# Whole 128-token chunks for group 0's attention, and group 2's attention moved to units 12 to 16

## The chip, the cores and the metric

The kernel runs on one core of one Trainium2 chip. The metric is the device time of one execution in microseconds. Before the change the median of three runs is 645.27 us (644.62 to 645.66).

Names of engines: PE (TensorE), ACT (ScalarE), DVE (VectorE), POOL (GpSimd), SP (the queue that issues nearly all DMAs). All five work through their own list of instructions strictly in order, and wait for each other by semaphores.

## The reference

Inputs: q, k, v of shape (4 batches, 8 heads, 768 positions, 64), a decay `lam` per head, and the weights of a gated layer. First a blocked linear attention with a running state, then RMS norm, then the gated layer:

```python
for b in range(nb):                       # blocks of 64 positions
    intra = (qb @ kb.T) * Dmask           # Dmask[i, j] = lam ** (i - j) for i >= j, else 0
    out = intra @ vb + (qb * lam ** (i + 1)) @ kv_state
    kv_state = lam ** 64 * kv_state + (kb * lam ** (63 - i)).T @ vb
x = out as (3072 tokens, 512)
xn = x / sqrt(mean(x * x) + 1e-6) * rms_g
y = (silu(xn @ w_gate) * (xn @ w_val)) @ w_out      # d_ff = 1536
```

The result does not depend on the block length: blocks of 128 positions with lam ** 128 between them compute the same.

## The kernel before

The 3072 tokens are six groups (m = 0 to 5) of 512. A group has four pairs of heads (p = 0 to 3), each pair filling the 128 partitions, and the layer's 1536 columns are twelve blocks of 128 (f). A unit is one group times one block: `gate` and `val` products into PSUM, silu and a multiplication, a split of the hidden values into a high and a low part, and `out` products into four accumulators. Units 0 to 5 are (0, f < 6), 6 to 17 are group 1, 18 to 23 are (0, f >= 6); from unit 24 on groups 2 to 5 run with a Strassen scheme (`strassen`, matmuls of L987), which needs sums of the group's rows (`Norm.sums`) and of the weights (`WeightSums`).

Before a group's units come its attention and its norm. The attention of one pair (class `Pair`) computes with 64x64 tiles, two blocks of 64 (o = 0, 1) in each chunk of 128 tokens:

- `scores` (L524, 16 matmuls), then `decay_a` on DVE (L540) multiplies with the mask, `decay_k` on ACT (L531) and `decay_q` on POOL (L544) scale k and q;
- `mix_chunks` (L604, 16 matmuls) and `state_sums` (L554, 16 matmuls);
- the states of the two blocks of a chunk are joined: `decay_sums` on ACT (L570), `whole_sums` on DVE (L573), `chain` over the chunks on DVE (L579), `middle` on DVE (L585), and `turn` on ACT (L592), which copies the halves across partitions;
- `mix_states` (L622, 14 to 16 matmuls), `keep_output` (L636, two ACT copies), `keep_squares` (L645).

Groups 0 and 1's attention and the conversion of the first seven weight blocks form the ramp. There the scheduler puts matmuls of `busy` (L141, tile `unread`) into PE's list wherever it expects a hole; they compute nothing. Group 0's norm (`row_sums` L667, `root` L691 on POOL, `spread` L700, `scaled` L753, `high` L758, `low` L761) ends in the first product of unit 0 (L800). Group 2's attention stands in units 16 to 19 of the list of steps, its norm in unit 21, and the scores of group 3's first pair in unit 23.

The order of all engines is made by a planner (`Plan.run`) at build time: every step has an engine, a cost, an `at` in units, what it reads and writes and which buffers it opens; a table `SHIFTS` moves the `at` of single steps. The planner lists the steps, and the emitted programs follow that list.

Loads of q, k, v and of weights share four buffers of 1 MB (`in`); from unit 24 on two of them hold the Strassen operands (`operand_tiles`). The group's rows x are kept in two buffers x0 and x1 (`SLOT_OF`).

Of the kernel before, what the change touches and what calls it, by code (L numbers as in the profile page):

```python
# [23 lines left out]
def retention_swiglu_kernel(  # L24
# [50 lines left out]
    lams, gcol = (cs[:, :NP], cs[:, NP : 2 * NP]), cs[:, 2 * NP :]  # L75
# [37 lines left out]
    pending = [(load_qkv, 1, 0), (load_gv, 1)]  # L113
# [42 lines left out]
    diagonal = const.tile([P, D], F32, name="diagonal")  # L156
    nc.gpsimd.tensor_add(diagonal, ident[:, :D], ident[:, D:])

    def powers(p, part):
        for s in range(2):  # L160
            lam = lams[s][:, p : p + 1].broadcast_to([P, D])
            if part == s:
                nc.vector.tensor_tensor_scan(
                    mask[:, p, s, :], lam, diagonal, 0.0, ALU.mult, ALU.add
                )
            elif part == 2:
                nc.vector.tensor_tensor_scan(
                    pw[:, p, s, :], lam, zeros, 1.0, ALU.mult, ALU.add
                )
        if part == 2:  # L170
            one = pw[:, p, 0, D - 1 :]
            nc.vector.tensor_mul(both[:, p : p + 1], one, one)
# [48 lines left out]
    zeros = wg[:, NF - 1, 1].bitcast(F32)[:, :D]  # L221
    nc.scalar.mul(zeros, ones[:, :D], 0.0)
# [272 lines left out]
    rows = {}  # L495
    xs = {}

    class Pair:
# [3 lines left out]
        def __init__(self, m, p):  # L502
            self.m, self.p = m, p
            if m == 0 and p % 2 or m == 1 and p == 0:
                self.pool, self.banks = ps_out, ("po0", "po1")
            elif m in (1, 2):
# [67 lines left out]

        def chain(self, chunks):
            for c in chunks:
                if c < GC - 1 and self.starts(c + 1):
# [3 lines left out]
                    both[:, self.p : self.p + 1], self.pst[1][:, c], ALU.mult, ALU.add,  # L581
# [45 lines left out]
        def keep_output(self, eng=nc.scalar):  # L627
            m, p = self.m, self.p
            if m not in rows:
                x = xpool.tile([P, NK, G], F32, tag=f"x{SLOT_OF[m]}", name=f"x_{m}")  # L630
                rows[m] = x, []
            x = rows[m][0]
# [15 lines left out]
        def add_squares(self, eng):  # L648
            sums = rows[self.m][1]
            s1 = sums.pop(1)  # L650
            eng.tensor_add(sums[0], sums[0], s1)

# [240 lines left out]

    def operand_tiles():
# [213 lines left out]
    units += [(m, f) for m in range(2, NG) for f in range(NF)]  # L1108
    SLOT_OF = {m: m % 2 if m < 2 else (m + 1) % 2 for m in range(NG)}
# [6 lines left out]
    class Plan:  # L1116
# [9 lines left out]
        SINGLE = {"row_sums", "spread", "quick", "largest_of_all"}  # L1126
# [4 lines left out]
            "quick": 16, "gate": 8, "val": 8, "part": 10, "out": 6, "add": 12, "first": 12, "second": 12,  # L1131
# [256 lines left out]
    def scale_steps(i, at):  # L1388
        step("DVE", 0.95, at, row_scales, slice(i * HALF, (i + 1) * HALF), w=[f"ts{i}"])

    def halve_steps(f, at):
# [7 lines left out]
        step("POOL", 1.28, at + 0.2, h.low, r=[f"rl{f}", f"rh{f}"], w=[f"w16_{f}:o"])  # L1399

    def sum_steps(f, at):
# [3 lines left out]
        for i in range(2):  # L1405
            step("POOL", 1.15, at + 0.1 * i, s.whole, i, tag, r=[f"w{'vg'[i]}{f}"], w=[f"r{f}:{i}"],
                 new=[] if i else [(f"r{f}", tag)])
        for i in range(2):
            step("DVE", 0.84, at + 0.5 + 0.1 * i, s.sums, i, to, r=[f"r{f}:0", f"r{f}:1"], w=[f"ws{f}"],
# [77 lines left out]

    def pair_scores(q, at):
# [511 lines left out]
```

## Time and profile before

| | us |
|---|---|
| median of three runs | 645.27 |
| the profiled execution | 644.94 |
| its span, first to last instruction | 643.2 |
| PE busy | 626.6 (97%) |
| DVE busy | 442.8 (69%) |
| ACT busy | 361.0 (56%) |
| POOL busy | 160.8 (25%) |

The span begins with the first instruction and ends with the landing of the last output; 1.7 us of the execution lie around it. Busy means that an instruction of the engine is under way. PE counts as busy in filler matmuls too. An idle time before an instruction is shown in square brackets with what ended it.

### The profile page before, as it was taken

What the parts mean: (1) busy time and instruction counts of PE and PEld (TensorE: products, weight loads), DVE (VectorE), ACT (ScalarE), POOL (GpSimd) and SP (SyncE); (2) the same over time, 40 slices, a digit from 0 to 9 for tenths busy, and PEclk for the clock granted to TensorE, in tenths of its full rate; (3) what the DMA queues carried; (4) which work ended last, traced back from release to release, by engine and by line L of the source; (5) the groups of instructions that cost most, each with busy time, mean ns of one, the idle gap of its engine ahead of it and who ended that gap; (6) DMA issues with size and microseconds to landing.
All of it is one profiled execution on the core that took longest, in us unless ns stands there. A gap on an engine that the chain in (4) does not pass through costs nothing.

```text
span 643.2 us, 15795 instructions
## 1 busy us (share of the span) xinstructions
PE 626.6 (97%) x6614; PEld 421.5 (66%) x6614; DVE 442.8 (69%) x892; ACT 361.0 (56%) x772; POOL 160.8 (25%) x166
## 2 busy tenths in 40 slices
PE   8899999999999999899999999999999999999997
PEld 5645564555556555677776777777777777777774
DVE  6698988789879867976678554498454488433434
ACT  4788877666856564465635455536454545433342
POOL 3213122000466763566601201112110102000000
PEclk9999999999999999999999999999999999999999
DMA  8738662540102400321200311200220000100001
GB/s 323 282 120 281 244 229 99 196 131 26 41 1 59 141 2 1 115 84 42 93 2 2 116 52 48 97 22 2 89 84 28 2 2 1 63 4 1 1 1 67
DMA packets 14327, 51.35 MB, mean 80 GB/s; under 512 B 1712, under 2 KB 1968, under 8 KB 12848
## 3 DMA queue, kind: packets, MB, share of 16 engines
q1 hardware_dynamic: 13968, 50.21, 22.5%
q8 instruction: 52, 0.85, 0.5%
q14 instruction: 19, 0.16, 0.1%
q10 hardware_dynamic: 288, 0.14, 0.1%
HBM read 44.05 MB, written 6.29 MB: 78 GB/s over the span
## 4 chain that ended last, share of the span: by engine, by line
PE 83%; DVE 9%; ACT 3%; issue 2%; DMA 1%; POOL 0%; DVEq 0%; ACTq 0%
PE pa L987 19%; PE pb L987 14%; PE acc L819 9%; PE acc L821 9%; PE acc L820 9%; PE pg L800 8%; PE pv L800 8%; PE pa L524 2%; PE po L604 2%; PE po L622 2%; PE po L554 1%; DVE a L579 1%; DVE x L761 1%; DVE a L540 1%; DMA qkv<-in_qkv_dram 1%
## 5 line engine op out<-in xcount | busy, mean ns | idle before, releaser
L821 PE MATMUL acc<-wo,hh 128*128 128x512 f16 (+1 forms) x288 | 110.2, 383 | 0.0
L820 PE MATMUL acc<-wo,hh 128*128 128x512 f16 (+1 forms) x288 | 110.1, 382 | 0.0
L1035 ACT COPY tx<-pa 128x256 f32<-128x256 f32 x144 | 53.1, 369 | 89.5 <-PE pa L987 66.0
L819 PE MATMUL acc<-wo,hh 128*128 128x512 f16 x216 | 82.0, 380 | 0.1
L1039 DVE TENSOR_TENSOR tx<-pb,tx 128x256 f32<-128x256 f32 x96 | 40.7, 424 | 56.0 <-PE pb L987 53.1
L800 PE MATMUL pv<-x,wv 128*128 128x512 f16 x288 | 69.0, 379 | 1.1 <-DVE sg L1068 1.1
L800 PE MATMUL pg<-x,wg 128*128 128x512 f16 x288 | 68.2, 379 | 0.9 <-ACT sg L1061 0.4
L987 PEld LDWEIGHTS <-wg 128*128 128x128 f16 x576 | 56.3, 98 | 17.8
L1080 ACT CAST hh<-sg 128x512 f16<-128x512 f32 (+2 forms) x73 | 44.6, 611 | 37.4 <-DVE sg L1055 25.4
L987 PEld LDWEIGHTS <-wo 128*128 128x128 f16 x576 | 55.8, 98 | 14.6 <-issue 1.3
L987 PEld LDWEIGHTS <-wv 128*128 128x128 f16 x576 | 56.1, 98 | 12.4 <-issue 1.2
L1043 DVE TENSOR_TENSOR sg<-pb,tx 128x256 f32<-128x256 f32 x48 | 20.3, 423 | 44.9 <-ACT tx L1035 34.1
L1091 DVE TENSOR_TENSOR hh<-sg,hh 128x512 f16<-128x512 f32 x53 | 43.1, 813 | 11.1 <-ACT hh L1080 10.9
L800 PEld LDWEIGHTS <-wg 128*128 128x128 f16 x288 | 27.1, 98 | 33.6 <-issue 2.1
L1055 DVE SCALAR_TENSOR_TENSOR sg<-tx,cv,sg 128x512 f32<-128x512 f32 (+1 forms) x49 | 38.0, 775 | 15.8 <-ACT sg L1047 12.2
L800 PEld LDWEIGHTS <-wv 128*128 128x128 f16 x288 | 26.5, 97 | 32.7 <-issue 2.3
L1047 ACT ACTIVATE sg<-sg,cg 128x256 f32<-128x256 f32 x48 | 24.4, 508 | 37.7 <-DVE sg L1043 37.6
L987 PE MATMUL pa<-x,wv 128*128 128x256 f16 x288 | 39.5, 273 | 0.9 <-DVE a L540 0.6
L987 PE MATMUL pb<-x,wv 128*128 128x256 f16 x288 | 39.4, 273 | 0.7 <-DVE x L761 0.7
L544 POOL TENSOR_TENSOR qkv<-qkv,pw 128x512 f32<-128x512 f32 x24 | 32.6, 1357 | 30.3 <-PE pa L524 28.1
L987 PE MATMUL pb<-tx,wo 128*128 128x256 f16 x288 | 39.3, 273 | 0.2 <-DVE tx L1039 0.2
L987 PE MATMUL pa<-x,wg 128*128 128x256 f16 x288 | 39.3, 273 | 0.0
(194 smaller groups left out, 1192.1 us busy)
## 6 DMA issues: line engine op xcount, KB each, us to landing
qkv<-in_qkv_dram SPq DMA_DIRECT2D x48, 512.0 KB, 5.2
raw_gv<-in_weights_dram SPq DMA_DIRECT2D x11, 1024.0 KB, 6.0
raw_o<-in_weights_dram SPq DMA_DIRECT2D x12, 512.0 KB, 5.0
out_dram<-o SPq DMA_DIRECT2D x23, 256.0 KB, 2.1
partial<-in_weights_dram SPq DMA_DIRECT2D x2, 512.0 KB, 11.9
out_dram<-o SPq DMA_DIRECT2D x1, 128.0 KB, 1.8
out_dram<-o ACTq DMA_DIRECT2D x1, 128.0 KB, 1.8
cs<-in_consts_dram ACTq DMA_DIRECT2D x1, 6.0 KB, 4.3
```

Source lines behind the costliest of these rows:

```text
L544: eng.tensor_mul(self.qT, self.qT, by.broadcast_to([P, GC, P]))
L800: nc.tensor.matmul(ps, w[:, kk, :], x[:, kk, :], start=i == kk == 0, stop=i == 2 and kk == NK - 1,)
L819: nc.tensor.matmul(acc[:, cols], hl[:, ts_], oh, start=first, stop=False, skip_group_check=True)
L820: nc.tensor.matmul(acc[:, cols], hh[:, ts_], ol, start=False, stop=False, skip_group_check=True)
L821: nc.tensor.matmul(acc[:, cols], hh[:, ts_], oh, start=False, stop=last, skip_group_check=True)
L987: nc.tensor.matmul(ps, w(ow, k), x(ox, k), start=first and i == k == 0, stop=i == 2 and k == 1, skip_group_check=True,)
L1035: nc.scalar.copy(self.kept[:, i], self.pa)
L1039: nc.vector.tensor_add(self.val[:, half], self.pb, self.kept[:, i])
L1047: nc.scalar.activation(self.sg[:, half], self.sg[:, half] if t else self.pa, AF.Silu, scale=cg[:, self.f, 0:1],)
L1055: nc.vector.scalar_tensor_tensor(sg, self.val[:, half], cv[:, self.f : self.f + 1], sg, ALU.mult, ALU.mult)
L1080: nc.scalar.copy(self.hh[:, half], self.sg[:, half])
L1091: nc.vector.tensor_sub(self.hl, self.sg, hh)
```

## The change

- Group 0 uses a class `Whole(Pair)`: one chunk of 128 tokens is one block. `all_scores` is 8 matmuls of 64 rows by 128 columns, `all_sums` 8, `all_mix` 8, `all_states` 6 (62 before, 30 now). `decay_sums`, `whole_sums`, `middle` and `turn` are not needed there; `decay_a` works on 128x512 elements in place of 128x256, and `keep_output` is one copy.
- The masks and powers are made 128 wide (`long_mask`, `long_pw`, in parts of the weight buffers that are not filled yet), and POOL and ACT copy the short ones out of them (`short_masks`, `short_powers`, `turned_powers`).
- Group 2's attention moves from units 16 to 19 to units 12, 13, 15 and 16, its norm from 21 to 19, group 3's first pair from 23 to 20. Group 2's rows lie in one of the four load buffers (`rows_of_loads`).
- Group 1's first pair, which was due before the first unit, is due after its start; the first weight block is loaded ahead of it (`pending`).
- Some costs of the planner change, and `SHIFTS` is a new table.

```diff
-    pending = [(load_qkv, 1, 0), (load_gv, 1)]
+    pending = [(load_gv, 1), (load_qkv, 1, 0)]
...
     def powers(p, part):
...
+        if part < 2:
+            h = 2 * p + part
+            nc.vector.tensor_tensor_scan(
+                long_mask[:, h, :], lam_b[:, h : h + 1].broadcast_to([P, P]), ident, 0.0,
+                ALU.mult, ALU.add,
+            )
+        else:
+            nc.vector.tensor_tensor_scan(
+                long_pw[:, p, :], lam_p[:, p : p + 1].broadcast_to([P, P]), zeros, 1.0,
+                ALU.mult, ALU.add,
+            )
+    def short_masks():
...
+        nc.gpsimd.tensor_copy(mask[one], by_pair[one, :, :, :D])
+        for s in range(2):
+            nc.gpsimd.tensor_copy(mask[two, :, s], by_pair[two, :, 1 - s, D:])
+    def short_powers():
+        nc.gpsimd.tensor_copy(pw[:, :, 0], long_pw[:, :, :D])
+        nc.gpsimd.tensor_copy(both, long_pw[:, :, P - 1])
+    def turned_powers():
+        for s, r in enumerate(lanes):
+            nc.scalar.copy(pw[r, :, 1], long_pw[lanes[1 - s], :, :D])
...
+    class Whole(Pair):
+        def all_scores(self, chunks):
...
+            for c in chunks:
+                for s, r in enumerate(lanes):
+                    nc.tensor.matmul(
+                        self.pa[s][:, c, :], self.kT[r, c, :], self.qT[r, c, :], start=True, stop=True
+                    )
+        def decay_a(self, s):
...
+            decay = long_mask[:, h : h + 1, :].broadcast_to([P, GC, P])
+            nc.vector.tensor_mul(self.a[:, s], self.pa[s], decay)
+        def all_sums(self):
...
+                    nc.tensor.matmul(
+                        self.pst[1][r, c, :], self.k[:, c, r], self.v[:, c, r], start=True, stop=True
+                    )
+        def all_mix(self, chunks):
...
+                    nc.tensor.matmul(
+                        self.po[r, c, :], self.v[:, c, r], self.a[:, s, c, :],
+                        start=c == 0, stop=False, skip_group_check=True,
+                    )
+        def all_states(self):
...
+                    nc.tensor.matmul(
+                        self.po[r, c, :], self.n[r, c, :], self.qT[r, c, :],
+                        start=False, stop=True, skip_group_check=True,
+                    )
...
+    def rows_of_loads(m):
+        rows[m] = stage.tile([P, NK, G], F32, tag="in", name=f"x_{m}", bufs=4), []
...
-        for p, at in enumerate((-0.85, 1.05, 1.95, 3.05)):
+        for p, at in enumerate((0.4, 1.05, 1.95, 3.05)):
             q = Pair(1, p)
...
-                n = u - (2 * NF - 8)
-                if 0 <= n < NP:
-                    q = Pair(2, n)
+                if u in (12, 13, 15, 16):
+                    q = Pair(2, (12, 13, 15, 16).index(u))
...
-                elif n == NP + 1:
+                elif u == 19:
                     norm_steps(2, u, 0.11)
-                if u == 2 * NF - 1:
-                    pair = Pair(3, 0)
-                    pair_scores(pair, u + 0.62)
+                if u == 2 * NF - 4:
+                    q = Pair(3, 0)
...
     SHIFTS = {
-        65: 4.35, 75: 8.3, 84: 0.45, 85: 4.3, 96: 4.25, 98: -3.65, 114: 4.7, 121: -0.4, 125: -8.4,
...
+        57: -5.4, 58: -2.7, 59: -4, 60: -4.9, 61: -1.2, 65: -0.6, 66: -7.9, 67: 3, 73: -3.85, 77:
...
```

What stands in the engines' lists. The number at the end of a name is a running number of the buffer; `a_0` is the attention tile of pair 0, `po` and `pst` are its outputs and state sums in PSUM, `qkv_1` the loaded q, k, v of pair 1.

DVE in the ramp, before the change, from the joining of pair 0's states of group 0:

```order
L573 TENSOR_TENSOR po_0_1_187<-a_0_179,po_0_1_187 128x256
L579 SCALAR_TENSOR_TENSOR a_0_179<-a_0_179,both,po_0_1_187 128x64 x3
L585 SCALAR_TENSOR_TENSOR a_0_179<-a_0_179,pw,po_0_0_186 128x256
L540 TENSOR_TENSOR a_1_257<-pa_1_0_227,mask 128x256
L579 SCALAR_TENSOR_TENSOR state<-a_0_179,both,po_0_1_187 128x64
```

DVE at the same place of the changed kernel, from pair 0's masking on:

```order
L698 TENSOR_TENSOR a_0_168<-pa_0_0_149,wv 128x512
L698 TENSOR_TENSOR a_0_168<-pa_0_1_150,wv 128x512
L159 SCALAR_TENSOR_TENSOR wv<-cs,ident 128x128
L601 SCALAR_TENSOR_TENSOR a_0_168<-a_0_168,wv,pst_0_174 128x64 x3
L207 TENSOR_REDUCE gmax<-pmax 128x1
```

The two operations around the chain (L573, L585) are gone, the maskings are twice as wide, and the chain stands directly behind them.

ACT in the ramp, before the change, for pairs 0 to 2 of group 0:

```order
L531 ACTIVATE qkv_0_96<-qkv_0_96,mask 128x4x64 x2
L570 ACTIVATE a_0_179<-po_0_0_186,pw 128x256
L531 ACTIVATE qkv_1_100<-qkv_1_100,mask 128x4x64 x2
L592 COPY a_0_179<-a_0_179 64x256 x2
L531 ACTIVATE qkv_2_103<-qkv_2_103,mask 128x4x64 x2
L636 COPY x_332<-po_0_0_186 128x4x64
L636 COPY x_332<-po_0_1_187 128x4x64
```

ACT at the same place of the changed kernel:

```order
L689 ACTIVATE qkv_0_96<-qkv_0_96,wv 128x4x64 x2
L689 ACTIVATE qkv_1_100<-qkv_1_100,wv 128x4x64 x2
L749 ACTIVATE sq_223<-po_0_185 128x512
L741 COPY x_225<-po_0_185 128x512
L689 ACTIVATE qkv_2_103<-qkv_2_103,wv 128x4x64 x2
L741 COPY x_225<-po_1_254 128x512
```

The scaling of the sums (L570) and the turned copies (L592) are gone, and the output is one copy.

PE ahead of the first product of unit 0, before the change (`pn` belongs to a weight's norm, `pr` is `spread`):

```order
L455 LDWEIGHTS ones_b
L455 MATMUL pn_1_674<-ssq_640,ones_b 128x1
L700 MATMUL pr_681<-ident,y_672 128x128 x4
L141 MATMUL unread_699<-ident 128x512
L622 MATMUL po_0_0_607<-qkv_0_429,a_0_570 64x64 x2
```

PE at the same place of the changed kernel, from the last two row sums of group 0:

```order
L766 MATMUL pss_238<-ones,sq_2_379 128x128 x4
L766 MATMUL pss_238<-ones,sq_3_394 128x128 x4
L141 MATMUL unread_418<-ident 128x256
L469 LDWEIGHTS ones_b
L469 MATMUL pn_420<-ssq_403,ones_b 128x2
L141 MATMUL unread_427<-ident 128x128
L799 MATMUL pr_429<-ident,y_415 128x128 x4
L543 MATMUL pa_0_0_443<-qkv_0_387 64x64
```

Before, group 1's pair 0 was finished here (L622); now only its scores (L543) stand ahead of the first product, and its other 46 matmuls come behind it.

DVE at the start of the Strassen units, before the change (`xt`, `yt`, `hy`, `xn` are scaled rows of group 2, the L761 writes are the low parts of its operands, L1068 and L1091 belong to units 22 and 23, L540 to group 3's pair 0):

```order
L1068 SCALAR_TENSOR_TENSOR sg_11_3150<-pv_11_3136,cv,sg_11_3150 128x512
L783 TENSOR_TENSOR xt_1_3164<-hy_3100 128x256
L784 TENSOR_TENSOR xt_1_3164<-xn_3_3142,hy_3100 128x256
L786 TENSOR_TENSOR xt_1_3164<-xn_3_3142,xt_1_3164 128x256
L787 TENSOR_TENSOR hy_3100<-xn_3_3142,xt_1_3164 128x256
L1091 TENSOR_TENSOR hh_11_3167<-sg_11_3150,hh_11_3167 128x512
L761 TENSOR_TENSOR x_2563<-yt_3101,x_2563 128x512
L540 TENSOR_TENSOR a_0_3206<-pa_0_0_3183,mask 128x256
L540 TENSOR_TENSOR a_0_3206<-pa_0_1_3184,mask 128x256
L867 SCALAR_TENSOR_TENSOR o_1_3212<-acc_6_1_2695,ik,partial 128x512
L761 TENSOR_TENSOR x_2563<-hy_3100,x_2563 128x512
L761 TENSOR_TENSOR x_2563<-xn_3_3142,x_2563 128x512
```

DVE of the changed kernel up to the first sum of unit 24 (L1141; L1036 to L1040 are sums of weights, L1170 and L1193 belong to units 22 and 23, L860 is the last low part):

```order
L860 TENSOR_TENSOR x_1780<-hy_2862,x_1780 128x512
L1170 SCALAR_TENSOR_TENSOR sg_10_2972<-pv_10_2974,cv,sg_10_2972 128x512
L297 SCALAR_TENSOR_TENSOR rest_h_3047<-wo_1673,ts,wo_10_2980 128x512
L1193 TENSOR_TENSOR hh_10_3029<-sg_10_2972,hh_10_3029 128x512
L1170 SCALAR_TENSOR_TENSOR sg_11_3092<-pv_11_3058,cv,sg_11_3092 128x512
L1141 TENSOR_TENSOR tx_2606<-pb_0_3103,tx_2605 128x256
```

The last low part of group 2's operands stood behind unit 23's operations; now it stands ahead of unit 22's, and group 3's pair 0 is no longer between them.

## Rows read from the trace of the kernel before

**Rows 1.** Page, part 1: PE's busy time over the whole span.
```profile
PE 626.6 (97%) x6614; PEld 421.5 (66%) x6614; DVE 442.8 (69%) x892; ACT 361.0 (56%) x772; POOL 160.8 (25%) x166
```

**Rows 2.** Windows: length, busy PE, PEld, DVE, ACT, POOL (instructions), PEclk, DMA.
```profile
5.00:39.05 34.05, 29.49 (x689) 21.30 (x690) 26.26 (x85) 24.87 (x58) 9.96 (x13) 1.00 0.84 317
39.05:75.00 35.95, 35.29 (x413) 19.68 (x412) 32.74 (x67) 29.37 (x58) 8.01 (x11) 1.00 0.63 227
119.00:205.00 86.00, 86.00 (x530) 49.57 (x529) 70.24 (x142) 59.13 (x108) 26.89 (x23) 1.00 0.18 60
205.00:262.00 57.00, 54.05 (x692) 28.76 (x691) 44.80 (x82) 31.38 (x65) 35.59 (x34) 1.00 0.18 57
```

**Rows 3.** Groups by form, PE, 5 to 39.05 us: count | busy, mean ns | idle.
```profile
L141 PE MATMUL unread<-ident 128*128 128x512 f32 x12 | 6.3, 619 | 0.0
L667 PE MATMUL pss<-ones,sq 128*128 128x128 f32 x32 | 4.6, 288 | 0.0
...
L141 PE MATMUL unread<-ident 128*128 128x256 f32 x6 | 2.3, 478 | 0.0
L141 PE MATMUL unread<-ident 128*128 128x384 f32 x4 | 1.7, 512 | 0.0
```

**Rows 4.** Chain of waits, 5 to 24 us: start, us, what.
```profile
4.96 1.13 PE pa L524 x32
...
19.91 0.48 ACT a L570
20.42 0.44 DVE po L573
...
21.90 0.49 DVE a L585
...
22.47 0.40 ACT a L592
```

**Rows 5.** Groups by form, DVE, whole span: count | busy, mean ns | idle.
```profile
L540 DVE TENSOR_TENSOR a<-pa,mask 128x256 f32<-128x256 f32 x48 | 18.3, 417 | 5.5 <-PE pa L524 4.4 <-DVE ws L938 0.5 <-PE po L622 0.3
L579 DVE SCALAR_TENSOR_TENSOR a<-a,both,po 128x64 f32<-128x64 f32 x64 | 17.2, 279 | 3.0
L753 DVE SCALAR_TENSOR_TENSOR xn<-x,gs,pr 128x512 f32<-128x512 f32 x8 | 5.6, 743 | 0.6 <-PE pr L700 0.6
```

**Rows 6.** Timeline, PE, end of the ramp: start, us, what.
```profile
31.28 1.16 PE L667 MATMUL pss<-ones,sq 128*128 128x128 f32 x8
39.05 1.12 PE L800 MATMUL pg<-x,wg 128*128 128x512 f16 x4
```

**Rows 7.** Chain of waits, 60 to 75 us: one pair's steps on PE.
```profile
65.32 0.62 PE po L604 x32
65.94 0.47 PE po L554 x32
70.61 0.62 PE po L622 x28
72.20 0.62 PE pa L524 x32
```

**Rows 8.** Timeline, PE, 260 to 272 us: the instructions that waited.
```profile
260.34 0.27 PE L987 MATMUL pa<-x,wv 128*128 128x256 f16 x1 [0.32 <-DVE x L761]
261.89 0.27 PE L987 MATMUL pb<-x,wv 128*128 128x256 f16 x1 [0.74 <-DVE x L761]
...
271.04 0.82 PE L987 MATMUL pa<-x,wv 128*128 128x256 f16 x6 [0.57 <-DVE a L540]
```

**Rows 9.** Timeline, all engines, from 254.7 us.
```profile
254.72 0.68 DVE L1091 TENSOR_TENSOR hh<-sg,hh 128x512 f16<-128x512 f32 x1
255.29 1.65 POOL L794 TENSOR_TENSOR tx<-xt,tx 128x768 f16<-128x768 f32 x1 [2.29 <-ACT tx L790]
255.32 2.16 DVE L761 TENSOR_TENSOR x<-yt,x 128x512 f16<-128x512 f32 x1
```

**Rows 10.** DMA issues: KB each, median us to landing.
```profile
qkv<-in_qkv_dram SPq DMA_DIRECT2D x48, 512.0 KB, 5.2
```

More of the change, by code (lines that the diff above doesn't have):

```diff
@@ L495, in retention_swiglu_kernel, with rows_of @@
     rows = {}
+    def rows_of(m):
+        if m not in rows:
+            rows[m] = xpool.tile([P, NK, G], F32, tag=f"x{ROWS_IN[m]}", name=f"x_{m}"), []
+        return rows[m]
     xs = {}
@@ L573, in whole_sums, with over_two @@
             nc.vector.tensor_add(self.pst[1], self.turned, self.pst[1])
+        def over_two(self):
+            return both[:, self.p : self.p + 1]
         def chain(self, chunks):
@@ L628, in keep_output @@
             m, p = self.m, self.p
[L629 to L632, printed above, removed]
+            x = rows_of(m)[0]
             copy = nc.scalar.copy if eng is nc.scalar else eng.tensor_copy
@@ L1124, in retention_swiglu_kernel @@
         }
-        SINGLE = {"row_sums", "spread", "quick", "largest_of_all"}
+        SINGLE = {
+            "row_sums", "spread", "quick", "largest_of_all", "all_scores", "all_sums", "all_mix", "all_states",
+        }
         TILED = {"scores", "state_sums", "mix_chunks", "mix_states"}
@@ L1130, in retention_swiglu_kernel @@
             "scores": 64, "mix_chunks": 64, "state_sums": 64, "mix_states": 60, "row_sums": 16, "spread": 16,
-            "quick": 16, "gate": 8, "val": 8, "part": 10, "out": 6, "add": 12, "first": 12, "second": 12,
+            "quick": 16, "all_scores": 16, "all_sums": 32, "all_mix": 16, "all_states": 24, "gate": 8, "val": 8, "part": 10, "out": 6, "add": 12, "first": 12, "second": 12,
         }
@@ L1583, in ramp_steps, with factor_of_x @@
                 w = f"pw{p}" if part == 2 else f"mask{2 * p + part}"
-                step("DVE", 0.56 if part == 2 else 0.28, -3.2 + 0.4 * p + 0.15 * (part == 2), powers, p, part, r=["cs"] + ["wg11"] * (part == 2), w=[w])
+                step("DVE", 0.38, -3.2 + 0.4 * p + 0.15 * (part == 2), powers, p, part, r=["cs"] + ["wg11"] * (part == 2), w=[w])
         ats = [-2.85, -2.3, -2.0, -1.75]
-        pairs = [Pair(0, p) for p in range(NP)]
-        for q, at in zip(pairs, ats):
-            pair_scores(q, at)
-            if q.p == 0:
-                step("PE", 0.3, -3.1, largest_of_all, r=["gmax", "pa0_0_0"], w=["pmax"], new=[("pmax", "po2")])
-                step("DVE", 1.33, -2.35, make_scales, r=["pmax"], w=["gs"])
-            pair_sums(q, at + 0.4)
-            pair_mix(q, at + 0.5)
+        def factor_of_x():
+            step("PE", 0.3, -3.1, largest_of_all, r=["gmax", "pa0_0_0"], w=["pmax"], new=[("pmax", "po2")])
+            step("DVE", 1.85, -2.35, make_scales, r=["pmax"], w=["gs"])
+        for p, at in enumerate(ats):
+            whole_pair(Whole(0, p), at, factor_of_x if p == 0 else lambda: None)
+        short = [f"mask{h}" for h in range(2 * NP)], [f"pw{p}" for p in range(NP)]
+        step("POOL", 1.6, -1.5, short_masks, r=short[0], w=["masks"])
+        step("POOL", 0.8, -1.5, short_powers, r=short[1], w=["pws"])
+        step("ACT", 0.8, -1.5, turned_powers, r=short[1], w=["pws"])
         first_norm_steps(0, -0.3, 0.05)
-        for p, at in enumerate((-0.85, 1.05, 1.95, 3.05)):
+        for p, at in enumerate((0.4, 1.05, 1.95, 3.05)):
             q = Pair(1, p)
@@ L1934, in turned @@
     def turned(a):
+        whole = G // D
         a = a.reshape(B, NP, 2, S // D, D, D).copy()
+        first = a[0, :, :, :whole].copy()
         a[:, :, :, 1::2] = a[:, :, ::-1, 1::2].copy()
+        a[0, :, :, :whole] = first
         return a
@@ L1965, in _consts @@
     import numpy as _np
-    halves = [_np.repeat(a, P // 2, axis=0) for a in (lam.reshape(-1, 2).T, lam.reshape(-1, 2).T[::-1])]
-    return _np.ascontiguousarray(_np.concatenate([*halves, rms_g.reshape(-1, P).T], axis=1))
+    rows = _np.broadcast_to(lam, (P, lam.shape[-1]))
+    halves = _np.repeat(lam.reshape(-1, 2).T, P // 2, axis=0)
+    return _np.ascontiguousarray(_np.concatenate([rows, halves, rms_g.reshape(-1, P).T], axis=1))
 def kernel(**inputs):
```

140 lines of the change are left out of this document (105 added, 35 removed), and 156 rows, old and new, of the table SHIFTS.

## The prediction

> **What bounds the kernel now.** I read the busy shares of the page first: PE is busy in 626.6 of 643.2 us [rows 1], so what a change can win is PE's waiting, its fillers, and its own work. The windows say where these lie. From 75 us on PE hardly stops; in the ramp, from 5.0 to 39.05 us, it is busy for 29.5 of 34.05 us [rows 2], and the groups by form show that 10.3 us of that are fillers in three forms [rows 3]. So 4.6 us of holes and 10.3 us of fillers, some 15 us, lie ahead of the first product. The chain of waits says what PE waits for there: pair after pair it leaves PE for ACT and DVE, through the joining of the two 64-blocks [rows 4]. Behind the first product DVE is the tight engine: 32.7 of 35.95 us until 75 us. Of the later holes the timeline shows four around the first Strassen units; three of them are 0.32, 0.74 and 0.57 us [rows 8], behind DVE. The granted clock reads 1.00 in all these windows [rows 2], so the work can be added in time units of one level, 2.4 GHz.
>
> **The change part by part.**
>
> *Group 0 on PE.* A pair's four steps cost 0.62 + 0.47 + 0.62 + 0.62 = 2.3 us before [rows 7], 62 matmuls. Now there are 30, none of which the trace shows: 22 with 128 columns that occupy half the array, and 8 with 64. Bounds by the nearest rows: a row sum, 128 columns on the full array, takes 4.6/16 = 0.29 us (each matmul is two records in f32) [rows 3]; a 64x64 matmul, a quarter of the array and 64 columns, takes 0.47/16 = 0.03 us, or 0.06 for 128 columns [rows 7]. Cost so goes with the share of the array that is occupied, and half an array should be near 0.14 for 128 columns: 22 x 0.14 + 8 x 0.07 = 3.6 us a pair, 1.3 more than before. At the low end (0.06) a pair is 1.6 us, at the high end (0.29, no overlap) 7.5 us. I take 3.6: 5.2 us more PE work over four pairs, and all of it in the ramp, where 15 us were empty.
>
> The Trainium skill's "TensorEngine Tiling (Array Packing)", Available Configurations, gives four tiles to the 64x64 mode and two to 64x128 and 128x64; an estimate from that, half of the full-array row for each of the 22, is the same 3.6 us. Its Key Properties add that a change of mode drains the engine, and the new forms bring three more modes; by that the ramp would lose a little, on which no row here has a price for the new pairs of modes.
>
> *Group 0 on DVE and ACT.* Out of each pair's path go L570 (0.48), L573 (0.44), L585 (0.49) and the two L592 (0.40 each): 2.2 us of latency [rows 4]. The masking doubles in size: from 18.3/48 = 0.38 to about 5.6/8 = 0.70 us, taking the 128x512 read from PSUM of L753 [rows 5]. The scans become 128 wide: a 64-wide operation is 17.2/64 = 0.27, and 256 more elements cost 0.32, so 64 more cost 0.08: 0.35 us each.
>
> *When the first product comes.* DVE's list up to pair 3's last state is now: 12 scans x 0.35 + 8 maskings x 0.70 + 16 chain steps x 0.27 + 8 small operations for the scales x 0.27 = 4.2 + 5.6 + 4.3 + 2.2 = 16.3 us. It starts when the first scores do, at 5.0 [rows 4], and I allow 1.5 us for waits on scores: 22.8. Then pair 3's states on PE (6 x 0.14 = 0.8), its square (0.6) and handoffs: its row sums start at 24.4. Before, they started at 31.28 and the first product at 39.05, 7.8 us later [rows 6]; the norm between the two is unchanged, so the first product comes at about 32.2; I say 32.5, since ten filler units (128x512 twice and 128x256) still stand ahead of it. That is 6.5 us earlier. But group 1's pair 0 has only its scores ahead of it now: 0.62 + 0.47 + 0.62 = 1.7 us of PE work [rows 7] move behind. On PE 4.8 us remain.
>
> *The limit by DVE behind it.* Pair 0 of group 1 also moves 2 x 0.38 + 4 x 0.27 + 0.44 + 0.49 = 2.8 us of DVE work into a stretch where DVE had 3.2 us of slack in 36. I take 1.3 us off for waits that this makes. **Ramp: -3.5 us.** Ends: -5.5 (quick forms, no DVE limit) and -0.5 (DVE gives nothing beyond the waits saved).
>
> *The short masks, scales and powers.* POOL and ACT copies, needed first by group 1; POOL is busy for 10 of 34 us there [rows 2], which covers them. Uncovered, about 2 us, inside the ends above. The new place of (1, 0)'s load behind a weight block is covered too, as that pair starts later.
>
> *Group 2's norm two units earlier.* Before, the low parts (L761) of group 2 came directly ahead of the products that read them, and took up to 2.16 us for work of 0.68 [rows 9]; now all stand ahead of unit 22's multiplication. The waits of 0.32, 0.74 and 0.57 us [rows 8] go: **-1.6 us**. Ends 0 and -2.3. What is late next there is the sum of the first Strassen products with a kept one, as in any unit.
>
> *Group 2's attention in units 12 to 16.* PE's work is the same. DVE gets 4 x 2.8 = 11 us in a stretch where it is busy for 70.2 of 86 us, with POOL at 26.9 [rows 2]; PE is busy for all 86 there, so nothing is to be won. Cover: DVE's 15.8 us of slack. I cost it at 0; ends 0 and +7 (the rival below). In return the stretch 205 to 262, with 3 us of PE idle, is relieved; the part I count is in the 1.6.
>
> *The load buffer.* With x in one buffer and the operands in two, group 3's pairs 1 to 3 share one. A pair's load (5.2 us to landing [rows 10]) can start only when the pair ahead has left it. In PE's new list a full Strassen unit and more stands between one pair's last states and the next one's scores, more than 7 us by the form of these units' work. I cost it at 0; ends 0 and +3.
>
> *Sum* against the profiled execution, 644.94 us (0.33 below the median): 644.94 - 3.5 - 1.6 = 639.8, and 640.2 against the median of the runs. **Forecast 640.2 us**, own range 637.8 to 642.8.
>
> **Rivals.**
>
> *DVE takes the ramp's gain.* For it: 91% busy behind the first product, and the conversions of the first weights stand in the same list whenever the rows come. Against it: DVE itself idles for 7.8 us of the ramp [rows 2], and some 3 of these go. If the ramp gives only 1 us and the Strassen start 1: 645.27 - 2 = 643.3.
>
> *Slower: DVE is overfull in units 12 to 16.* One mechanism: DVE operations with two SBUF inputs that meet a POOL operation are held. Row: L761 took 2.16 us beside a POOL operation that began 0.03 us ahead of it, where the like L1091 took 0.68 [rows 9]. Group 2's attention brings POOL four scalings of q, three additions of squares and small copies into the stretch, some 11 us; if each holds DVE for its whole length, DVE needs 70.2 + 11 + 11 = 92 of 86 us, PE waits 6 us there, and the later norm and halves slip, so that the 1.6 are not won: 640.2 + 6 + 1.6 = 647.8. It decides once the held time passes the 4.6 us of slack that are left. Against it: in 205 to 262 the same attention stood beside more POOL work (35.6 of 57 us) and PE lost 3 us in all. The Trainium skill's "SBUF — State Buffer" says of the shared port pair of the two engines that it is locked for a whole instruction and the loser blocks fully; by that rule every meeting costs in full, which is this rival's price, and rows 9 agree with it for one meeting.
>
> *The new forms do not overlap.* Then a pair is 7.5 us, 21 us more in all; 15 empty us take up some 9 of them beside the waits that remain: 640.2 + 12 = 652. Nothing in the rows speaks for it; the 64x64 forms do overlap.
>
> **How the numbers follow.** Forecast 0.67, DVE takes the gain 0.16, DVE overfull 0.13, no overlap 0.02, the rest (unforeseen waits from the new order, or more gain) 0.02. About 0.2% (1.3 us) is what a measurement of this kernel can tell from no change. The forecast's case is faster throughout; of the second rival 643.3 lies beyond the bound of 644.0, with some of its spread not, so 0.10 faster and 0.06 same. The third is slower. Faster 0.77, same 0.08, slower 0.15. For the range I go from 636.5 (both gains at their ends) to 646.5, which takes in the second rival and the milder half of the overfull DVE, and leaves out 0.13.
>
> **What would show it.** Right: the first product between 31 and 34 us; fillers of about 5 us in the ramp; a pair's new steps at 3 to 4 us of PE; L570, L573, L585 and L592 absent until group 1; no holes behind group 2's low parts; DVE below 97% between the start of unit 11 and unit 17. Wrong: a first product after 36 us; PE waits of over 1 us in total on DVE's multiplications or attention in units 12 to 18; scores of group 3's pairs that wait for a DMA; DVE waiting less than 1 us between 33 and 70 us while PE waits more than 3.

## The result, and the profile after

The changed kernel takes 637.29 us (median of 4 runs, 636.78 to 637.75), the one before 645.46 us beside it (4 runs, 644.62 to 645.92): a ratio of 0.9875, 95% interval 0.9857 to 0.9892, 8.2 us less. The forecast was 640.2 us; the sign and, in the main, the mechanism hold, and the gain is 1.6 times the forecast. The measured time lies 0.5 us below the sum's own range (637.8 to 642.8) and inside the wider one (636.5 to 646.5). The profiled execution has a span of 635.0 us, against 643.2.

Part 1 of the page of the changed kernel, as [rows 1]: PE has 2.2 us less to do and waits 6.0 us less (10.6 us in place of 16.6).

```profile
PE 624.4 (98%) x6346; PEld 421.3 (66%) x6346; DVE 440.1 (69%) x876; ACT 357.3 (56%) x758; POOL 161.6 (25%) x170
```

Windows of the changed kernel (length, busy PE, PEld, DVE, ACT, POOL, granted clock, DMA), as [rows 2]. The ramp now ends at 30.84 us, and PE idles for 0.9 us in it where it idled for 4.6; behind it PE idles for 1.6 us until 75 us, where DVE is busy for 40.0 of 44.2; from 75 to 400 us for 1.1 us in all, before 5.4 us.

```profile
5.11:30.84 25.73, 24.84 (x328) 20.23 (x329) 21.48 (x60) 16.48 (x34) 10.34 (x16) 1.00 1.02 390
30.84:75.00 44.16, 42.52 (x589) 24.20 (x588) 40.01 (x87) 38.41 (x77) 7.39 (x13) 1.00 0.61 216
75.00:119.00 44.00, 44.00 (x235) 25.90 (x233) 38.52 (x76) 32.08 (x61) 5.99 (x5) 1.00 0.50 180
119.00:205.00 86.00, 85.40 (x867) 50.25 (x866) 71.88 (x145) 62.26 (x121) 37.81 (x35) 1.00 0.16 51
205.00:262.00 57.00, 56.72 (x416) 30.68 (x414) 44.90 (x80) 28.53 (x56) 32.94 (x30) 1.00 0.15 52
262.00:400.00 138.00, 137.82 (x1691) 101.28 (x1690) 92.17 (x182) 73.97 (x174) 46.93 (x49) 1.00 0.19 64
```

The chain of waits of the changed kernel from 14 to 24 us, as [rows 4] (start, us, what). Where the chain before left PE four times in the ramp for DVE, ACT or POOL, it now stays on PE from 7.6 to 23.2 us: scores (L683), sums (L714), mix (L724), states (L734) and row sums (L766) follow each other without a gap. Its steps also price a pair: 2 x 0.65 + 0.62 + 1.02 + 0.80 = 3.7 us.

```profile
13.78 1.02 PE po L724 x16
14.80 0.65 PE pa L683 x8
15.45 0.80 PE po L734 x12
16.25 0.62 PE pst L714 x16
16.87 1.11 PE pa L683 x16
17.98 1.09 PE pss L766 x8
```

PE's timeline in the changed kernel at the end of the ramp, as [rows 6], with the square of pair 3 on ACT. The 16 row sums from 23.12 are those of pairs 2 and 3 (each pair has 8 records). Pair 3's can't start before its square ends at 23.83; the ninth record starts at 24.11. Before, pair 3's eight records stood alone at 31.28. The first product comes at 30.84 (before 39.05): 8.2 us earlier, and 6.7 us behind pair 3's row sums (before 7.8). Its second part then waits 0.73 us for the low part of the weights.

```profile
23.12 2.05 PE L766 MATMUL pss<-ones,sq 128*128 128x128 f32 x16
23.23 0.60 ACT L749 ACTIVATE sq<-po 128x512 f32<-128x512 f32 x1 [0.74 <-PE po L734]
...
26.87 1.16 PE L799 MATMUL pr<-ident,y 128*128 128x128 f32 x8 [0.24 <-POOL y L790]
...
28.09 2.72 DVE L852 SCALAR_TENSOR_TENSOR xn<-x,gs,pr 128x512 f32<-128x512 f32 x4
...
30.84 1.05 PE L899 MATMUL pg<-x,wg 128*128 128x512 f16 x4
...
33.48 1.90 PE L899 MATMUL pg<-x,wg 128*128 128x512 f16 x8 [0.73 <-DVE wg L491]
```

### The profile page after: what moved, and what is told of

It is laid out like the page before. It is cut to its first block, busy times and chain, and to the rows that moved or that the text cites. A ratio compares the mean times of both kernels' runs of the same rounds, so it can differ in the third digit from the quotient of the medians.

```text
span 635.0 us, 15236 instructions
## 1 busy us (share of the span) xinstructions
PE 624.4 (98%) x6346; PEld 421.3 (66%) x6346; DVE 440.1 (69%) x876; ACT 357.3 (56%) x758; POOL 161.6 (25%) x170
## 4 chain that ended last, share of the span: by engine, by line
PE 88%; DVE 5%; ACT 3%; DMA 2%; issue 1%; DVEq 0%; ACTq 0%
PE pa L1089 20%; PE pb L1089 15%; PE acc L918 10%; PE acc L920 9%; PE acc L919 9%; PE pv L899 8%; PE pg L899 8%; PE po L626 2%; PE pa L543 2%; PE po L644 2%; DMA raw_o<-in_weights_dram 2%; PE po L573 1%; ACT junk L464 1%; DMA cs<-in_consts_dram 1%; PE po L724 1%
## 5 line engine op out<-in xcount | busy, mean ns | idle before, releaser
L1141 DVE TENSOR_TENSOR tx<-pb,tx 128x256 f32<-128x256 f32 x96 | 40.7, 424 | 61.7 <-PE pb L1089 56.0
L1089 PEld LDWEIGHTS <-wg 128*128 128x128 f16 x576 | 55.9, 98 | 16.6 <-issue 0.5
L563 POOL TENSOR_TENSOR qkv<-qkv,pw 128x512 f32<-128x512 f32 x20 | 27.0, 1351 | 112.8 <-PE pa L543 97.5
L1157 DVE SCALAR_TENSOR_TENSOR sg<-tx,cv,sg 128x512 f32<-128x512 f32 (+1 forms) x49 | 39.8, 811 | 17.0 <-ACT sg L1149 13.3
L1193 DVE TENSOR_TENSOR hh<-sg,hh 128x512 f16<-128x512 f32 x53 | 42.7, 805 | 10.4 <-ACT hh L1182 9.7
L1149 ACT ACTIVATE sg<-sg,cg 128x256 f32<-128x256 f32 x48 | 24.4, 508 | 38.9 <-DVE sg L1145 38.7
L1089 PE MATMUL pb<-x,wg 128*128 128x256 f16 x288 | 39.3, 273 | 0.3 <-DVE sg L1145 0.3
L1089 PE MATMUL pa<-tx,wo 128*128 128x256 f16 x288 | 39.3, 273 | 0.0
```

Source lines behind the costliest of these rows:

```text
L563: eng.tensor_mul(self.qT, self.qT, by.broadcast_to([P, GC, P]))
L1089: nc.tensor.matmul(ps, w(ow, k), x(ox, k), start=first and i == k == 0, stop=i == 2 and k == 1, skip_group_check=True,)
L1141: nc.vector.tensor_add(self.val[:, half], self.pb, self.kept[:, i])
L1149: nc.scalar.activation(self.sg[:, half], self.sg[:, half] if t else self.pa, AF.Silu, scale=cg[:, self.f, 0:1],)
L1157: nc.vector.scalar_tensor_tensor(sg, self.val[:, half], cv[:, self.f : self.f + 1], sg, ALU.mult, ALU.mult)
L1193: nc.vector.tensor_sub(self.hl, self.sg, hh)
```

## The experiments

In the first three the two orders are crossed: the program's list is cut at one gate product, with one kernel's order ahead of it and the other's behind it. In place of the planner, `follow` takes the first step of a given ranking whose inputs and buffers are there. The later experiments that add or move steps use it too, so the rest of every list stays that of the changed kernel.

### The ramp alone

```
-        order = plan.run()
+        order = plan.follow(RANK, AT)   # changed kernel's list to unit 6's gate, then that of before
```

> The changed kernel's order on every engine up to the first gate product of unit 6 (whole chunks for group 0, new first pair of group 1), and the order of the kernel before from there on, with group 2's attention, norm and buffers as before. Theory A (two separate gains): the first product comes near 31 us as in the changed kernel, and of these 8.2 us some 1.7 go to the moved pair, 1.0 to new waits on DVE until 75 us and up to 0.9 to PE work that the trace shows as longer; so 4.6 to 5.5 us faster than before, 640 to 641 us, and the holes at unit 20 to 24 (0.32, 0.74, 0.57 us behind the low parts and a masking) are there again. Rival B (the whole gain is the ramp's): 8 us faster, about 637.3 us. The forecast's own term for this part was 3.5 us, 641.9 us.

Measured: 639.42 us, ratio 0.9917 (0.9900 to 0.9933), 5.3 us less than before. The first product comes at 30.73 us. The holes behind the low parts stand again, and so does the one before a Strassen product, as PE's timeline of this kernel shows:

```profile
206.08 1.89 PE L899 MATMUL pv<-x,wv 128*128 128x512 f16 x8 [1.12 <-DVE sg L1170]
255.51 0.27 PE L1089 MATMUL pa<-x,wv 128*128 128x256 f16 x1 [0.32 <-DVE x L860]
257.07 0.27 PE L1089 MATMUL pb<-x,wv 128*128 128x256 f16 x1 [0.74 <-DVE x L860]
...
266.21 0.82 PE L1089 MATMUL pa<-x,wv 128*128 128x256 f16 x6 [0.57 <-DVE a L559]
...
346.11 0.81 PE L1089 MATMUL pa<-tx,partial 128*128 128x256 f16 x6 [1.11 <-ACT tx L1137]
```

Theory A holds: of 8.2 us, 2.9 are given back behind the first product. The forecast's 1.7 + 1.3 for that was right as a sum.

### The later part alone

```
-        order = plan.run()
+        order = plan.follow(RANK, AT)   # list of before to a gate of unit 6 (or 2), then the changed one's
```

> The order of the kernel before up to the first gate product of unit 6 (group 0 in 64x64 tiles), and the changed kernel's order from there on (group 2's attention in units 12 to 16, its rows in a load buffer, its norm earlier, the new shifts). Theory A: the first product at 39 us as before, the holes behind the low parts gone, PE waits of about 1.3 us in all from 75 us on in place of 5.4: 3.5 us faster than before, about 642 us. Rival B: no faster than before, 645.4 us. The forecast's term for this part was 1.6 us, 643.8 us; the rival of an overfull DVE in units 12 to 16 would make it slower than before.

> As f2_late_only, with the seam where the two orders differ by fewer steps: the order of the kernel before up to the first gate product of unit 2, the changed kernel's order from there on. In f2_late_only TensorE waited 2.78 us at the seam for one weight block's norm and ran at a granted clock of 0.67 in the 5 us around it, which alone would hide a gain. Theory A: without such a seam the late part is worth what f1_ramp_only lacks against the changed kernel, about 2.7 us: 642 us. Rival: the late part gives nothing without the new ramp, within 0.5 us of the kernel before.

Measured: the cut at unit 6 gives 646.89 us, ratio 1.0028 (1.0014 to 1.0042); the cut at unit 2 gives 642.16 us, ratio 0.9955 (0.9942 to 0.9968). The first says nothing of the change: at its seam PE waits 2.78 us for a weight block's squares, and the windows of 1 us behind it (same columns as above) show what follows that wait, a granted clock of 0.50, which is 1.2 GHz:

```profile
101.00:102.00 1.00, 0.00 (x0) 0.00 (x0) 0.81 (x2) 0.97 (x4) 0.00 (x0) 0.85 0.77 123
102.00:103.00 1.00, 0.82 (x3) 0.28 (x3) 0.55 (x5) 1.00 (x3) 0.00 (x0) 0.50 0.57 180
103.00:104.00 1.00, 1.00 (x4) 0.44 (x3) 1.00 (x3) 1.00 (x3) 0.00 (x0) 0.50 0.99 410
104.00:105.00 1.00, 1.00 (x4) 0.32 (x3) 1.00 (x3) 0.71 (x2) 0.00 (x0) 0.50 0.76 320
```

With the better seam the later part is worth 2.6 us. Alone, the two parts give 5.3 + 2.6 = 7.9 us, together 8.2: they add up within the intervals (some 1 us each). Units 2 to 5 stand in the changed order in both runs; the cut at unit 2 gains nothing there (PE waits 0.78, 0.35 and 0.52 us from 45 to 75 us, the kernel before 0.30).

### Which engine sets the new ramp

```
+        for i in range(4):
+            step("DVE", 0.38, 0.0, powers, 0, i % 2, w=["again"])    # ahead of pair 3's masking
```
```
+        step("PE", 1.1, 0.0, busy, 4, w=["unread"])                  # behind pair 3's state sums
```

> The changed kernel with four scans more on DVE (masks of pair 0 computed again, the same values, some 1.4 us) ahead of pair 3's masking. Theory P (TensorE's own work now sets the row sums of pair 3): DVE's masking and sums of pair 3 have over 1 us to spare, so the first product moves by 0 to 0.4 us and the time by as much, 637.3 to 637.7 us. Theory D (DVE's list sets them, as the forecast reckoned): the first product comes 1.4 us later, and the time is 638.7 us.

> The changed kernel with four filler units more on TensorE (one 128x512 product in f32 of two records, some 1.1 us) behind pair 3's state sums. Theory P: every one of these 1.1 us shows, the first product comes 1.1 us later, 638.4 us. Theory D: they fall into a time in which TensorE waits for DVE anyway, and the time stays within 0.2 us of 637.3.

Measured: with 1.4 us more on DVE 637.52 us (ratio 0.9883, 0.9868 to 0.9898) and the first product at 31.43, 0.6 us later; with 1.1 us more on PE 637.76 us (0.9890, 0.9874 to 0.9906) and the first product at 32.07, 1.2 us later. So PE sets the ramp, and DVE has 0.8 us to spare, less than the 1 us of theory P: the two engines end close to each other. The times, with intervals of 1 us on either side, can't tell how much of either delay arrives at the end.

### The joining put back

```
+        def again(self, which):
+            sums, n = self.pst[1], self.n
+            if which == 0:
+                nc.scalar.copy(sums, sums)
+            elif which == 1:
+                nc.vector.tensor_copy(sums, sums)
+            elif which == 2:
+                nc.vector.scalar_tensor_tensor(n, n, 1.0, n, ALU.mult, ALU.max)
+            else:
+                for r in lanes:
+                    nc.scalar.copy(n[r], n[r])
```

> The changed kernel with the four joining steps of the 64x64 tiles put back into every pair of group 0 as steps that change nothing: a copy of the state sums in place on ACT, one on DVE ahead of the chain, then the chain's states through DVE (128x256, two SBUF inputs) and in two halves through ACT; 2.2 us of path a pair, 3.7 us of DVE in all. TensorE keeps its 30 matmuls a pair. Theory J (the joining is what kept the first product back): DVE's 3.7 us less the 0.8 us that g1_dve_more showed to be spare at least, and up to 8 us if every pair's path shows; first product at 34 to 39 us, time 639.5 to 643. Rival (the order hides the path and TensorE sets the ramp): first product up to 1 us later, time below 638.2.

> As j1_joined_again, with the two ACT steps alone (0.47 and 2 x 0.40 us a pair of path, nothing more on DVE). If the length of the path counts: the first product comes 0.9 us or more later, up to 3.6 us if all four pairs show. If only DVE's occupied time counts: it moves by less than 0.5 us and the time stays within 0.4 us of 637.3.

Measured: all four steps 645.91 us, ratio 1.0012 (1.0000 to 1.0025); the first product comes at 39.85 us, 0.8 us later than before the change. ACT's two alone 641.74 us, ratio 0.9943 (0.9925 to 0.9960); first product 35.16 us. PE's timeline with all four:

```profile
11.22 1.29 PE L746 MATMUL po<-qkv,a 64*64 64x128 f32 x12 [1.10 <-ACT a L728]
...
19.47 1.20 PE L746 MATMUL po<-qkv,a 64*64 64x128 f32 x12 [2.30 <-ACT a L728]
20.60 1.51 PE L714 MATMUL pst<-qkv 128*64 128x64 f32 x16
22.04 2.08 PE L683 MATMUL pa<-qkv 64*128 64x128 f32 x16
...
30.71 1.29 PE L746 MATMUL po<-qkv,a 64*64 64x128 f32 x12 [1.31 <-ACT a L728]
```

This is theory J, beyond its upper end: the states of three pairs (L746 here) wait for the last copy, and behind the wait of 2.30 us the sums take 1.51 us and the scores 2.08 where the changed kernel has 0.69 and 1.18, at a granted clock of 0.50:

```profile
21.00:22.00 1.00, 1.00 (x14) 0.93 (x14) 1.00 (x3) 1.00 (x3) 0.02 (x1) 0.50 0.39 41
```

So of the 9.0 us by which the first product is later than in the changed kernel, 4.7 are these three waits and 1.7 the halved clock, which the kernel before, with an order made for the joining, did not have there. With ACT's part alone, which adds nothing to DVE, half of the loss is there. PE's timeline of that run shows two kinds of wait, for the last copy (L728) and for ACT's scaling of k (L689), which stands behind the copies in ACT's list:

```profile
16.69 1.20 PE L746 MATMUL po<-qkv,a 64*64 64x128 f32 x12 [0.72 <-ACT a L728]
...
22.32 0.62 PE L714 MATMUL pst<-qkv 128*64 128x64 f32 x13 [0.96 <-ACT qkv L689]
...
26.02 1.29 PE L746 MATMUL po<-qkv,a 64*64 64x128 f32 x12 [0.32 <-ACT a L728]
```

So the length of the path and the time of ACT both count, and this run doesn't part them. In this order of PE, the joining takes the whole of the ramp's gain with it; PE's own forms, which are the same here, bring none. What the forms would bring in an order planned for the joining is not shown. (The time ends near that of before although the later part's 2.6 us are kept, since the moved pair still gives back its 3.)

### Twice the matmuls

```
-                    nc.tensor.matmul(
-                        self.pa[s][:, c, :], self.kT[r, c, :], self.qT[r, c, :], start=True, stop=True
-                    )
+                    for i in range(0, P, D):
+                        nc.tensor.matmul(
+                            self.pa[s][:, c, i : i + D], self.kT[r, c, :], self.qT[r, c, i : i + D],
+                            start=True, stop=True,
+                        )
...
```

> The changed kernel with every matmul of group 0's attention cut into two of half the columns (60 of a pair in place of 30, nearly the 62 of the kernel before); DVE, ACT and POOL do the same work. Theory J (what the whole chunks save is the joining of two blocks on DVE and ACT): TensorE's time for a pair stays near 3.7 us, and the time within 0.4 us of 637.3. Theory F (a part of it is the fetching of TensorE's instructions, on which the ramp of before waits 1.4 us in all): waits of TensorE for issue come back, 0.6 us and more each, and the time is 638.5 to 640 us.

Measured: 644.83 us, ratio 0.9979 (0.9961 to 0.9997), in two groups: five runs from 640.99 to 641.62, seven from 644.81 to 646.18. Even the lower group is some 4 us above the changed kernel, so both theories fall. No wait for issue came back, and PE has no gap; it is busy for longer. PE's timeline of this kernel:

```profile
4.86 3.73 PE L684 MATMUL pa<-qkv 64*128 64x64 f32 x32
...
9.67 1.94 PE L717 MATMUL pst<-qkv 128*64 128x32 f32 x32
11.40 2.00 PE L729 MATMUL po<-a,qkv 128*64 128x64 f32 x32
13.33 1.16 PE L684 MATMUL pa<-qkv 64*128 64x64 f32 x16
...
22.75 1.15 PE L717 MATMUL pst<-qkv 128*64 128x32 f32 x32
23.82 2.05 PE L684 MATMUL pa<-qkv 64*128 64x64 f32 x32
```

The 16 half scores of a pair take 2.0 us where the 8 whole ones take 1.3 (2 x 0.65 above), so half the columns cost 0.12 to 0.14 us in place of 0.16. A pair comes to some 5.1 us in place of 3.7.

In this execution, one of the upper group, the first pair's steps took nearly twice as long as later ones: 3.66 us for the scores (4.86 to 8.52), then 1.94 and 2.00 where later pairs have 1.15 and 1.20. The granted clock reads 1.00 there, but only because its record in the trace starts later: the first entry, a rise to full speed, is at 13.26 us, and the view counts what lies ahead of it as 1.00. In the changed kernel's trace the first entry is at 5.83 us, in all others between 5.0 and 7.7. Half speed for 7.4 us more costs an estimated 3.7 us, and the medians of the two groups, 641.3 and 645.1, are 3.8 apart. That the lower group had its rise early is not shown, since none of its runs was profiled.

### The fillers

```
-                if spare_bank and idle > 0.5:
+                if spare_bank and idle > 0.5 and now < 5:
```

> The changed kernel without the fillers behind 5 us (4.1 us of TensorE time in the ramp, of which 0.6 + 0.5 and 2.4 stand around the norm). The forecast counted fillers as empty time: by that the first product still comes at 30.8 us and the time stays within 0.3 us of 637.3. Rival: with waits of some 2 us in their place the granted clock falls and what follows runs at 1.2 GHz for some us, as behind the wait of 2.78 us in f2_late_only: 1.5 to 4 us slower, 639 to 641 us, with a granted clock under 0.9 between 25 and 40 us.

Measured: 636.84 us, ratio 0.9874 (0.9861 to 0.9887), as the changed kernel; first product at 29.57 us with one matmul and 30.83 with the rest. PE's waits of up to 0.98 us in the fillers' place leave the clock where it was, as the window shows, PE busy for 5.8 of 10 us:

```profile
25.00:35.00 10.00, 5.83 (x59) 2.99 (x56) 9.17 (x20) 8.14 (x17) 4.06 (x5) 1.00 0.73 292
```

So these fillers were rightly counted as empty time.

### Three waits filled

```
+low(0)  wg_0              (DVE)
 low     x_0, rows 1 and 2
-low(0)  wg_0
...
-norm_bank pn_4            (PE)
 gate(2) pg_3
+norm_bank pn_4
...
-gate(2) pg_18             (PE)
 mix_chunks, state_sums po_2_3; out(0) acc_1_0
+gate(2) pg_18
 out(2)  acc_1_2
```

> The changed kernel with three instructions moved in its order, each behind a wait of TensorE that its trace shows: on DVE the first weights' low part ahead of the low parts of x (wait of 0.73 us at 33.48), on TensorE the norm of weight block 4 behind the next gate product (0.64 us at 66.69), and unit 18's last gate product ahead of the output products that wait for a low part (0.60 us at 198.14). If the waits are simply filled: 1.5 to 2.0 us less than the changed kernel, about 635.5 us. Rival: what is moved back on one engine makes a new wait behind it, 637.0 to 637.6 us.

Measured: 637.75 us, ratio 0.9889 (0.9876 to 0.9902): no gain. Each wait came back near its old place (at 33.48, 66.69 and 198.14 us), as PE's timeline shows; 0.73 became 0.57, 0.64 became 0.46, 0.60 became 0.69, all behind DVE:

```profile
34.88 1.04 PE L899 MATMUL pv<-x,wv 128*128 128x512 f16 x4 [0.57 <-DVE wv L491]
...
67.87 0.69 PE L543 MATMUL pa<-qkv 64*64 64x64 f32 x30 [0.46 <-DVE e L476]
195.59 0.62 PE L626 MATMUL po<-a,qkv 64*64 64x64 f32 x26 [0.69 <-DVE en L356]
```

### More on DVE in units 10 to 17

```
+        for i in range(8):
+            step("DVE", 0.7, 0.0, more, w=["first"])                 # two ahead of each masking of group 2
```

> The changed kernel with eight more DVE reductions of 0.68 us (5.4 us in all, no one reads them), two ahead of the masking of each pair of group 2. The forecast gave DVE 15.8 us of slack here before the attention came in and 4.6 us in its rival's worst case; the changed kernel's trace shows DVE busy for 71.9 of 86 us from 119 to 205 us. By that trace 5.4 us fit: within 0.5 us of 637.3. By the rival (DVE nearly full there): TensorE waits on DVE's multiplications and low parts, 638.5 to 641 us.

Measured: 637.85 us, ratio 0.9889 (0.9871 to 0.9907), an interval that holds the changed kernel's 0.9875. Its window, with DVE at 74.4 us and PE waiting 1.9 us against 0.6:

```profile
119.00:205.00 86.00, 84.14 (x832) 48.66 (x831) 74.36 (x153) 60.27 (x117) 33.29 (x31) 1.00 0.18 61
```

So 5.4 us more of DVE's work cost PE some 1.3 us of waits there, and the difference of the ratios, 0.0014 or 0.9 us, is within the intervals: between the two expectations. The profiled execution is the slowest of the six (640.17 us), but the rest of its loss lies ahead of this window, with one wait of 1.92 us at 68 us. By this one trace the stretch is not full, but it holds less than the 14 idle us of the changed kernel's window suggest.

## Why the prediction was right, and where it was off

**The first product.** Forecast 32.5, measured 30.84, just ahead of the band of 31 to 34. The working had DVE's list end at 22.8 us and pair 3's row sums start at 24.4. They started at 24.1, so this step came out nearly to the number, but by luck: DVE's list, pair 3's last state included, ended at 21.0 us (5.27 to 21.03, busy for 14.1 us where 16.3 were summed), and the runs with more on DVE and more on PE show that PE, with hardly a gap from 5.1 to 25.6 us, sets this time. What made the first product early is the stretch behind it. The prediction called the norm unchanged, 7.8 us; it took 6.7. Before, the joining of group 1's pair 0 stood in DVE's list between `spread` (`pr`) and the scaling of the rows (`xn`), and its states and the fillers stood ahead of the first product in PE's; the change moved that pair, as the prediction itself says a little later. Timeline of the kernel before, to be read beside the lines of the changed one above:

```profile
27.67 1.16 PE L667 MATMUL pss<-ones,sq 128*128 128x128 f32 x8
...
34.20 1.16 PE L700 MATMUL pr<-ident,y 128*128 128x128 f32 x8 [0.20 <-POOL y L691]
...
35.22 0.48 DVE L585 SCALAR_TENSOR_TENSOR a<-a,pw,po 128x256 f32<-128x256 f32 x1
...
35.80 2.72 DVE L753 SCALAR_TENSOR_TENSOR xn<-x,gs,pr 128x512 f32<-128x512 f32 x4
```

From `pr` to `xn` it is 1.2 us now and was 1.6; from `xn` to the first product 2.75, before 3.25. So the 1.7 us of difference are, rounded, 0.3 of the row sums, 1.0 of the norm, and the 0.3 added for ten filler units, which the run without fillers shows to cost nothing.

**A pair on PE, and the fillers.** A pair was forecast at 3.6 us and measured 3.7; fillers of about 5 us were named as a sign, and the ramp holds 4.1 (2.0 + 1.2 + 0.9 in three forms). The joining steps, now L589, L592, L607 and L614, begin with group 1. The estimate from the Trainium skill's "TensorEngine Tiling (Array Packing)", Available Configurations, gave the same 3.6 by halves of the array, and the trace agrees in the sum, with 0.16 us for a score, 0.13 for a mix and 0.13 for a state matmul against 0.14. But the rule that cost goes with the share of the array does not hold. The six state matmuls are 64x64 tiles (L734 above), a quarter of the array, and not half of it as the prediction counted them: by its rule they would cost 0.06 us each and a pair 3.2. And a score matmul of half the columns cost 0.12 to 0.14 us at half the work. The new forms are two modes more, not three (64x128 and 128x64), and no gap shows where PE goes from one form to the next.

**What is given back behind it.** 1.7 us of moved PE work and 1.3 of waits on DVE were forecast, 3.0 in all; the ramp alone gives 8.2 - 5.3 = 2.9. The waits stand where they were put: 1.6 us of PE idle until 75 us against 0.7, and filling them only moved them. So the term "Ramp: -3.5 us" was mis-sized by its first number alone: -5.3 measured, just within its ends. The range is luck in part: both gains at their ends give 645.27 - 5.5 - 2.3 = 637.5, not the 636.5 that the prediction puts there, and the measured 637.29 lies between the two.

**The joining.** The 2.2 us of latency that leave each pair's path were named and priced, but the sum was then made from DVE's list. Putting the steps back costs 8.6 us. That this is near four times 2.2 is chance, since it is made of 4.7 us of waits at three pairs, 1.7 of halved clock and the longer lists; but latency was a term to sum in its own right.

**The Strassen start.** Forecast -1.6, measured -2.6 (later part alone) to -2.7 (the difference of the two ratios 0.9917 and 0.9875). The three waits went as said. Of the timeline's other holes two were in view and left out of the sum: 1.12 us behind DVE's multiplication, in the stretch that group 2's attention has left, and 1.11 us at a product ahead of group 3. Both come back with the order of before (206.08 and 346.11 above). The second has a cause that the rival of the overfull DVE names. Timeline of the kernel with the ramp alone:

```profile
342.95 1.64 POOL L893 TENSOR_TENSOR tx<-xt,tx 128x768 f16<-128x768 f32 x1 [23.65 <-ACT tx L889]
342.97 2.17 DVE L1157 SCALAR_TENSOR_TENSOR sg<-tx,cv,sg 128x512 f32<-128x512 f32 x1
```

An operation of 0.75 us (the median of its line in either kernel) takes 2.17 beside a POOL operation that began 0.02 us ahead, as in [rows 9], and the copies behind it are late. The Trainium skill's "SBUF — State Buffer", Who interferes with whom, says that the loser of the shared port pair blocks for a whole instruction; the rows agree to within 0.2 us (the held operation ends 0.55 us behind POOL's). But such time is hardly less now: from 100 us on 18 DVE operations of 128x512 take over 1.25 us, 14.7 us above 0.7 each, against 16 and 15.0 before. They only stand less often where PE waits.

**Group 2's attention in units 12 to 16, and the load buffer.** Cost 0 was right. PE waits there once, for 0.60 us, behind a low part that met a POOL operation; timeline of the changed kernel:

```profile
196.24 1.29 POOL L302 TENSOR_TENSOR wo<-rest_h,rest_l 128x512 f16<-128x512 f32 x1 [2.08 <-ACT wg L1054]
...
196.68 1.41 DVE L1193 TENSOR_TENSOR hl<-sg,hh 128x512 fp32r<-128x512 f32 x1
...
198.14 0.50 PE L918 MATMUL acc<-wo,hl 128*128 128x512 f32 x1 [0.60 <-DVE hl L1193]
```

From unit 11's start to unit 17 (131.7 to 190 us) DVE is busy for 48.2 of 58.3 us (83%), below the 97% that would have shown the rival. No scores of group 3 wait for a DMA.

**The clock.** The prediction read 1.00 in every window and so added all work at one level. In the kernel before, too, the record starts only at 7.67 us: the 32 records of the first scores take 1.13 us there, 0.64 later. That is half a microsecond at the head of the ramp, with no part in the sum.

What stays open: how much of the later 2.6 us is owed to the moved attention and how much to the new shifts; norm 2 can't go ahead of its own attention, and no run parted the two.

## What to carry to other kernels

Where one engine's list is fixed and takes small chains in turn, count the hand-offs of a chain times its number before counting anyone's busy time: put back, four steps of under half a microsecond at each of four pairs cost 4.7 us of waits and 8.6 us in all. When work is moved out of a stretch, size the whole stretch again, what is called unchanged too. The three waits behind the tight engine that were filled here came back beside their old place; it may be better to take operations off that engine, which no run here tried. And before reading an experiment that joins two orders, look at its seam.

## What the runs showed of the hardware

- A wait of PE of 2.30 us in the ramp was followed by a granted clock of 0.50 (1.2 GHz) from 21 to 24 us, one of 2.78 us by the same from 102 to 105 us, one of 1.95 us (ACT's part alone, at 73 us) by the same from 75 to 78 us. One of 1.92 us (more on DVE, at 68 us) left the clock at 1.00, and so did several of up to 0.98 us with PE busy for 5.8 of 10 us. Where the clock fell, a part of a wait's cost stands behind it, in rows of work that seem slow.
- The granted clock reads 1.00 also ahead of its first entry in the trace. In the run with twice the matmuls that entry, a rise, comes at 13.26 us, and the 32 score records ahead of it take 3.73 us where 2.05 are usual.
- Halving a matmul's columns took only a fifth off its cost in the 64x128 form (0.16 to about 0.13 us), but nearly half in the 128x64 form of the mix (0.13 to 0.07 us).
- In the ramp before, PE waited 0.6 and 0.8 us for issue, with no semaphore behind it, as its timeline shows; with 30 matmuls a pair, and with 60 of half the columns, no such wait is left.

```profile
14.22 0.39 PE L622 MATMUL po<-qkv,a 64*64 64x64 f32 x11 [0.64 <-issue]
...
19.26 0.57 PE L554 MATMUL po<-qkv 64*64 64x64 f32 x22 [0.77 <-issue]
```
